# The output projection of an attention and SwiGLU kernel as seven block products instead of eight, with an order of work written out in full

## The chip, the cores and the metric

The kernel runs on one core of one Trainium2 chip. The metric is the device time of one execution in microseconds (us); the kernel before takes 381.37 us, the median of three runs (381.36 to 381.74). PE is TensorE (matrix products), DVE is VectorE, ACT is ScalarE, POOL is GpSimd, SP is SyncE, which here only issues transfers.

## The reference, cut to what matters

Attention with a decay for 8 batches of 8 heads, 576 tokens and 64 columns per head; its output, seen as 4608 tokens of 512 columns, goes through an RMS norm and a gated feed-forward layer. The change concerns the last product alone.

```
scores = scale * q @ k.T + decay; causal mask; softmax; attn @ v     # 8 x 8 heads, 576 tokens
xn = x / rms * rms_g                                                 # 4608 x 512
silu * val = silu(xn @ w_gate) * (xn @ w_val)                        # 4608 x 1536
out = (silu * val) @ w_out                                           # 4608 x 512
```

## The kernel before, in words

**Two halves, woven together.** The attention half works batch by batch. It loads q, k and v through POOL's queue, turns q and k (DMA transposes on SP's queue, the first ones on PE), and scales v (`scale_v`, L444, on DVE for the first two batches and on POOL for the others). Scores are matrix products into the two `sc` banks (L469), ACT takes the exponential (L487), POOL masks the diagonal block (`affine_select`, L494), PE multiplies by v (L513), DVE divides by the row sum (L527, L529), and `norm` makes the normed rows and turns them (L545 to L578).

The feed-forward half works on 9 groups of 512 tokens. Groups 0 to 7 are the first 512 tokens of the batches, group 8 gathers the last 64 tokens of all eight. `gate` (L615) makes one 128-column slice of the hidden layer for 512 tokens: four matmuls with `w_gate` and four with `w_val` (L624), each with 128 partitions, a 128-column stationary operand and 512 moving columns; a tanh on ACT (L636); two element-wise steps on DVE (L638 makes `ga`, L631 writes the slice of `hT` in bf16). There are 12 slices per group. In groups 0 and 1 a unit is 16 matmuls of 128 moving columns, so that the work can begin with the first 128 tokens. The norm's gains are multiplied into the weights on the way (L358, DVE).

`project` (L643) is the part that is changed. For 128 tokens it sums 12 matmuls in one PSUM bank: `hT` is the stationary operand (128 by 128) and `wo` the moving one (512 columns). The 12 come in three parts of four. ACT copies the bank to `ores` (L662), and SP's queue stores 128 tokens of 2 KB rows (L666, for group 8 L675). There are four such calls per group, 36 in all.

**Buffers.** All feed-forward products, and the values and transposes of the attention, share a ring of four PSUM banks `ff`. A gate slice takes two of them, one until L638 is done and one until L631 is done. `hT` has two buffers: a group's gates can't begin before the projection of the group two ahead of it has read its last block.

**What sets the order.** `Plan` (L41) holds every piece of work as a unit with an engine, an estimated duration, a key, its predecessors and the ring slots that it takes and gives back. `Plan.run` (L83) plays the units against these durations: an engine that is free takes the ready unit with the lowest key. The order in which units start there is the order in which instructions are written to each engine's queue, and the chip keeps that order on each engine. Before the play, 26 seeds shake the keys (L93 to L99). The durations steer the order only; on the chip an instruction waits for its real predecessors.

## Time and profile before

| What | Value |
|---|---|
| time, median of three runs | 381.37 us |
| span of the profiled execution, first to last instruction | 380.4 us |
| PE busy | 356.9 us in 3894 matmuls |
| DVE, ACT, POOL busy | 219.5, 237.9, 199.9 us |
| granted TensorE clock, mean | 0.996 |

The profiled execution's own time isn't given apart from its span; the span plus what lies around it (start and end of the execution) is what the runs time, and the median stands 0.97 us above the span. A row of the profile names a group of instructions by line, engine, operation and tiles, then how many there were, their busy time and mean duration, and after a bar the time for which the engine stood idle just ahead of them and what ended it. Matmuls are pipelined: a row's mean duration is longer than the distance at which they follow each other. In the table by stages, each engine has its busy time in that stretch and, in brackets, how many instructions.

### The profile page before, as it was taken

What the parts mean: (1) busy time and instruction counts of PE and PEld (TensorE: products, weight loads), DVE (VectorE), ACT (ScalarE), POOL (GpSimd) and SP (SyncE); (2) the same over time, 40 slices, a digit from 0 to 9 for tenths busy, and PEclk for the clock granted to TensorE, in tenths of its full rate; (3) what the DMA queues carried; (4) which work ended last, traced back from release to release, by engine and by line L of the source; (5) the groups of instructions that cost most, each with busy time, mean ns of one, the idle gap of its engine ahead of it and who ended that gap; (6) DMA issues with size and microseconds to landing.
All of it is one profiled execution on the core that took longest, in us unless ns stands there. A gap on an engine that the chain in (4) does not pass through costs nothing.

```text
span 380.4 us, 9641 instructions
## 1 busy us (share of the span) xinstructions
PE 356.9 (94%) x3894; PEld 213.6 (56%) x3942; DVE 219.5 (58%) x458; ACT 237.9 (63%) x378; POOL 199.9 (53%) x280
## 2 busy tenths in 40 slices
PE   2699999899979999999999999999999999999994
PEld 2489875698854455445555555555545544444441
DVE  6658999775645547454745565546654654554430
ACT  5676678789868576857695769566965443331321
POOL 8966589799998656964598449831302000000000
PEclk9999999999999999999999999999999999999998
DMA  9999999999999999993999499972120210100004
GB/s 124 211 215 212 218 136 216 160 156 159 151 142 141 154 115 134 178 161 62 137 150 173 80 138 143 179 92 56 36 57 30 55 34 29 55 28 29 28 30 110
DMA packets 128869, 44.84 MB, mean 118 GB/s; under 512 B 117300, under 2 KB 121912, under 8 KB 128824
## 3 DMA queue, kind: packets, MB, share of 16 engines
q0 software_dynamic: 76368, 23.34, 62.1%
q1 hardware_dynamic: 52376, 20.74, 30.2%
q8 instruction: 31, 0.51, 0.6%
q10 hardware_dynamic: 80, 0.13, 0.2%
q14 instruction: 14, 0.11, 0.1%
HBM read 37.90 MB, written 9.44 MB: 124 GB/s over the span
## 4 chain that ended last, share of the span: by engine, by line
PE 81%; DVE 7%; DMA 6%; POOL 3%; issue 2%; ACT 1%; POOLq 0%; ACTq 0%
PE ff L624 45%; PE ff L649 22%; PE ff L513 7%; PE sc L469 6%; DMA v<-in_v_dram 3%; DMA qk<-in_q_dram 2%; DVE wg L358 2%; DVE x L529 1%; DVE wv L358 1%; DVE hT L631 1%; POOL v L339 1%; DVE Vs L444 1%; DVE Vs L445 1%; DVE ga L638 1%; POOL qk L328 0%
## 5 line engine op out<-in xcount | busy, mean ns | idle before, releaser
L638 DVE SCALAR_TENSOR_TENSOR ga<-th,ff 128x512 f32<-128x512 f32 x108 | 73.5, 683 | 85.2 <-ACT th L636 83.7
L636 ACT ACTIVATE th<-ff 128x512 f32<-128x512 f32 x108 | 64.2, 595 | 73.0 <-PE ff L624 56.6
L649 PE MATMUL ff<-wo,hT 128*128 128x512 bf16 x409 | 105.3, 379 | 0.8 <-issue 0.2
L487 ACT ACTIVATE PT<-sc 128x1024 bf16<-128x1024 f32 x96 | 95.0, 1017 | 9.9 <-PE sc L469 9.7
L624 PE MATMUL ff<-xT,wg 128*128 128x128 bf16 (+1 forms) x655 | 97.2, 288 | 3.7 <-issue 1.9
L624 PE MATMUL ff<-xT,wv 128*128 128x128 bf16 (+1 forms) x665 | 96.9, 287 | 1.7 <-DVE x L529 0.8
L631 DVE SCALAR_TENSOR_TENSOR hT<-ga,ff 128x512 bf16<-128x512 f32 x108 | 72.9, 684 | 19.6 <-PE ff L624 17.0
L624 PEld LDWEIGHTS <-wg 128*128 128x128 bf16 x720 | 54.0, 99 | 39.1 <-issue 2.9
L624 PEld LDWEIGHTS <-wv 128*128 128x128 bf16 x720 | 53.2, 98 | 36.7 <-issue 1.3
L649 PEld LDWEIGHTS <-hT 128*128 128x128 bf16 x432 | 40.5, 98 | 45.5
L494 POOL TENSOR_SCALAR_AFFINE_SELECT PT<-PT 128x1024 bf16<-128x1024 bf16 x32 | 35.6, 1112 | 49.2 <-ACT PT L487 49.2
L513 PEld LDWEIGHTS <-PT 128*128 128x128 bf16 x896 | 37.9, 99 | 12.7 <-POOL PT L494 0.2
L513 PE MATMUL ff<-Vs,PT 128*128 128x65 bf16 x896 | 42.6, 195 | 0.1
L444 POOL TENSOR_TENSOR Vs<-v,decT 128x512 bf16<-128x512 f32 (+1 forms) x30 | 31.4, 1048 | 15.7 <-DMA v<-in_v_dram 14.0
L662 ACT COPY ores<-ff 128x512 f32<-128x512 f32 (+1 forms) x36 | 20.9, 580 | 29.8 <-PE ff L649 29.0
L469 PE MATMUL sc<-QT,KT 64*128 64x128 bf16 (+1 forms) x960 | 34.1, 213 | 2.5 <-ACT PT L487 1.7
L339 POOL DMA_DIRECT2D v<-in_v_dram x39 | 34.5, 887 | 2.9 <-DVE rden L527 1.1
L529 DVE TENSOR_TENSOR x<-ff,rden 128x256 f32<-128x256 f32 (+1 forms) x80 | 33.8, 422 | 2.8
L469 PEld LDWEIGHTS <-KT 64*128 64x128 bf16 x960 | 24.6, 96 | 15.0 <-issue 11.5
L527 DVE RECIPROCAL rden<-ff 128x4 f32<-128x4 f32 (+1 forms) x80 | 14.1, 176 | 30.5 <-PE ff L513 30.5
L545 ACT ACTIVATE junk<-x 128x512 bf16<-128x512 f32 (+1 forms) x40 | 25.1, 627 | 9.7 <-DVE x L529 8.9
L316 POOL DMA_DIRECT2D qk<-in_q_dram x34 | 29.9, 882 | 1.8 <-DMA qk<-in_k_dram 0.9
(63 smaller groups left out, 221.3 us busy)
## 6 DMA issues: line engine op xcount, KB each, us to landing
out_dram<-ores SPq DMA_DIRECT2D x32, 256.0 KB, 3.8
v<-in_v_dram POOLq DMA_DIRECT2D x31, 256.0 KB, 6.0
qk<-in_k_dram POOLq DMA_DIRECT2D x26, 128.0 KB, 5.6
qk<-in_q_dram POOLq DMA_DIRECT2D x26, 128.0 KB, 4.8
wv<-in_moe_w_val_dram POOLq DMA_DIRECT2D x3, 512.0 KB, 13.0
wg<-in_moe_w_gate_dram POOLq DMA_DIRECT2D x3, 512.0 KB, 11.2
wo<-in_moe_w_out_dram POOLq DMA_DIRECT2D x2, 768.0 KB, 16.1
v<-in_v_dram POOLq DMA_DIRECT2D x8, 128.0 KB, 7.6
```

The source lines that it names most:

```text
L339: queue.dma_start(out=T_v32[h.slot][0:n, :, :], in_=v[b, :, p0:p0 + n, :].rearrange("h p d -> p h d"))
L444: eng.tensor_tensor(T_Vs[hv.slot][0:n, j, :, 0:D], T_v32[h.slot][0:n, :, :], bcast(dj, D), ALU.mult)
L469: nc.tensor.matmul(t[:, par, c:c + n], lhsT=kt[r, p, kj * 128:(kj + 1) * 128], rhs=qt[r, p, qi * 128:qi * 128 + n], start=True, stop=True)
L487: nc.scalar.activation(T_of_p[hp.slot][:, 0:2 * half].rearrange("p (a c) -> p a c", a=2)[:, :, 0:cols], T_sc[h.slot][:, :, 0:cols], ACT.Ex ...
L494: nc.gpsimd.affine_select(out=d, in_=d, pattern=[[0, 8], [1, n]], compare_op=ALU.is_ge, fill=0.0, base=0, channel_multiplier=-1)
L513: nc.tensor.matmul(po[:, p, :], lhsT=T_of_p[h.slot][:, c:c + 128], rhs=vs[:, kj, 2 * p + par, :], start=(kj == 0), stop=(kj == qi))
L529: nc.vector.tensor_tensor(d, po[:, :, 0:D], bcast(r, D), ALU.mult)
L624: nc.tensor.matmul(T_ff[h.slot][:, c:c + n], lhsT=w[:, dc, fc * 128:(fc + 1) * 128], rhs=xT[:, dc, t0:t0 + n], start=(dc == 0), stop=(dc = ...
L631: nc.vector.scalar_tensor_tensor(hT, in0=three[0], scalar=0.5, in1=three[1], op0=ALU.mult, op1=ALU.mult)
L636: th = act(0.6, key - 0.1, lambda: nc.scalar.activation(T_th[ht.slot], T_ff[hg.slot], ACT.Tanh, scale=0.5), [ug], take=[ht])
L638: a = dve(0.69, key - 0.1, lambda: nc.vector.scalar_tensor_tensor(T_ga[ha.slot], in0=T_th[ht.slot], scalar=1.0, in1=T_ff[hg.slot], op0=ALU ...
L649: nc.tensor.matmul(T_ff[hf.slot], lhsT=T_hT[hold_hT[g].slot][:, fc, j * 128:(j + 1) * 128], rhs=wo[:, fc, :], start=(fc == 0), stop=(fc == ...
```

## The change

**The product.** For each group of 512 tokens the hidden block (512 tokens by 1536) is cut into 2 by 2 blocks of 256 tokens by 768, and `w_out` into 2 by 2 blocks of 768 by 256. Seven block products replace eight. Each is 12 matmuls of 256 moving columns: two halves of 128 tokens, 6 slices of the hidden dimension, both halves in one PSUM bank. DVE makes four sums or differences of hidden blocks per group (`s1` to `s4`, each 128 partitions by 1536 elements, bf16, from SBUF to SBUF; `s3` overwrites a block of `hT`) and once, for the whole kernel, four of weight blocks (`combine`). The results are put together as they leave PSUM: two copies on ACT and five additions of an SBUF tile and a bank on DVE (`plus`). Two products are summed onto a bank that has been copied out already (`m2` on `m1`, `m3` on `m5`).

**The stores.** A store now takes 256 tokens by 256 columns, in rows of 1 KB, four per group (group 8: eight). All go through SP's queue; before, the very last one went through ACT's.

**The order.** The seeds are gone. `ORDER` gives each of the 1797 units its rank as two letters, in the order in which units are created, and the play uses the ranks as keys. Ring slots and predecessors are as before, `ores` has five buffers instead of three, and a ring `sm` of three holds the block sums. Some estimated durations are set anew: loads through POOL, and the weights' scaling at 2.0 instead of 1.3.

**A shared tile.** The buffers `qk2`, which the first two batches use to turn q and k on PE, now lie inside the tile `wt` that later takes the combined weights.

```diff
-SEEDS = (37914, 460032, 76309, 917069, 999632, 56819, 902762, 379427, 333574, 378073, 410848, 600471, 719706,
...
+LETTERS = string.digits + string.ascii_letters
+ORDER = (
+    "0e1q020d000b0c080j0406030i0a0u0w0l0m0q0r0x090o0E0H0I070p010h050g0f0t0k0y0n0J0s0O0v0T0F1b0K1e0A0W0P1h"
...
+        for u, a, b in zip(self.units, ORDER[::2], ORDER[1::2]):
+            u.key = LETTERS.index(a) * len(LETTERS) + LETTERS.index(b)
...
+    wt = sb.tile([128, 3, NFC // 2, DM // 2], BF16, name="wt")
+    flat = wt.rearrange("p k f d -> p (k f d)")
+    T_qk2 = [flat[:, i * 1024:(i + 1) * 1024].rearrange("p (h r d) -> p h r d", h=H, r=2) for i in range(sizes["qk2"])]
...
+    T_sm = ring("sm", sizes["sm"], [128, NFC // 2, GT // 2], BF16)
...
-            Lw[nm, i] = [dve(1.3, key, emit, deps[nm])]
+            Lw[nm, i] = [dve(2.0, key, emit, deps[nm])]
...
+    def combine(deps):
+        def add(name, out, a, b, *need):
+            Lt[name] = dve(0.95, 0.85, lambda: nc.vector.tensor_tensor(out, a, b, ALU.subtract), list(need))
+        add("t1", wt1, w12, w11, Lo[0], *deps)
+        add("t3", w12, w22, w12, Lo[1], Lt["t1"])
+        add("t2", wt2, w22, wt1, Lt["t1"], Lo[1])
+        add("t4", wt4, w21, wt2, Lt["t2"])
...
-    def project(g, j, key):
...
+    def project(g, key, sums):
...
+        def s1():
+            nc.vector.tensor_tensor(T_sm[h1.slot], blocks()[2], blocks()[3], ALU.add)
...
+        u1 = dve(0.95, sums, s1, done[1], take=[h1], give=[hs])
+        u3 = dve(0.95, sums + 0.001, s3, [u1] + done[0], give=[hs])
+        u2 = dve(0.95, sums + 0.002, s2, [u1] + done[0], take=[h2], give=[hs, h1])
+        u4 = dve(0.95, sums + 0.003, s4, [u2], take=[h4], give=[hs, h2])
...
+        def product(a, w, hf, deps, take=(), give=(), more=False):
+            def emit():
+                t = T_ff[hf.slot]
+                for s in range(2):
+                    for fc in range(HF):
+                        nc.tensor.matmul(t[:, s * HD:(s + 1) * HD], lhsT=a()[:, fc, s * 128:(s + 1) * 128],
+                                         rhs=w[:, fc, :], start=(not more and s == 0 and fc == 0), stop=(s == 1 and fc == HF - 1),
...
+            return pe(1.315, key(n[0] - 1), emit, deps, take=list(take), give=list(give))
...
+        m1 = product(lambda: blocks()[0], w11, f1, done[0] + [Lt["t1"]], take=[f1], give=[hs])
+        v1 = copy(f1, A, [m1], take=[A])
+        m2 = product(lambda: blocks()[1], w21, f1, done[0] + [v1, Lo[1]], give=[hs], more=True)
+        store(E, 0, 0, copy(f1, E, [m2], take=[E], give=[f1]))
+        m6 = product(lambda: T_sm[h2.slot], wt2, f2, [u2, Lt["t2"]], take=[f2], give=[h2])
+        v2 = plus(f2, A, A, [m6, v1], give=[f2])
+        m7 = product(lambda: blocks()[2], w12, f3, [u3, Lt["t3"]], take=[f3], give=[hs])
+        v3 = plus(f3, A, Bb, [m7, v2], take=[Bb], give=[f3])
+        m5 = product(lambda: T_sm[h1.slot], wt1, f4, [u1, Lt["t1"]], take=[f4], give=[h1])
+        v4 = plus(f4, Bb, C, [m5, v3], take=[C])
+        store(C, 1, 1, v4)
+        m3 = product(lambda: T_sm[h4.slot], w22, f4, [m5, v4, u4], give=[h4], more=True)
+        store(A, 0, 1, plus(f4, A, A, [m3, v3], give=[f4]))
+        m4 = product(lambda: blocks()[3], wt4, f5, done[1] + [Lt["t4"]], take=[f5], give=[hs])
+        store(Bb, 1, 0, plus(f5, Bb, Bb, [m4, v4], give=[f5]))
```

## The prediction on record

> **What bounds the kernel now.** I read the page first: how busy each engine is, and which of them the chain that ended last runs through.
>
> ```profile
> span 380.4 us, 9641 instructions
> ...
> PE 356.9 (94%) x3894; PEld 213.6 (56%) x3942; DVE 219.5 (58%) x458; ACT 237.9 (63%) x378; POOL 199.9 (53%) x280
> ...
> PE 81%; DVE 7%; DMA 6%; POOL 3%; issue 2%; ACT 1%; POOLq 0%; ACTq 0%
> PE ff L624 45%; PE ff L649 22%; PE ff L513 7%; PE sc L469 6%; DMA v<-in_v_dram 3%; DMA qk<-in_q_dram 2%; DVE wg L358 2%; DVE x L529 1%; DVE wv L358 1%; DVE hT L631 1%; POOL v L339 1%; DVE Vs L444 1%; DVE Vs L445 1%; DVE ga L638 1%; POOL qk L328 0%
> ```
>
> PE is on the chain for 81% of the span, and the line that is changed (L649) for 22%. An average hides stages, so the table by stages comes next. Its columns are the stretch, its length, and the busy time of PE, PEld, DVE, ACT and POOL.
>
> ```profile
> 0.00:10.30 10.30, 3.57 (x38) 2.71 (x38) 6.18 (x26) 5.62 (x7) 9.10 (x17) 1.00 1.19 141
> 10.30:39.00 28.70, 24.73 (x434) 22.31 (x432) 19.93 (x44) 19.28 (x30) 21.11 (x29) 1.00 1.35 208
> 39.00:76.50 37.50, 33.95 (x622) 26.64 (x623) 33.27 (x74) 28.14 (x41) 28.33 (x35) 1.00 1.71 182
> 76.50:141.00 64.50, 62.06 (x914) 43.94 (x920) 36.88 (x80) 50.21 (x83) 56.04 (x81) 1.00 1.44 145
> 141.00:180.00 39.00, 38.66 (x377) 20.52 (x384) 21.43 (x44) 27.61 (x44) 26.27 (x36) 1.00 1.09 135
> ...
> 297.00:364.70 67.70, 67.33 (x343) 31.36 (x349) 35.85 (x57) 22.24 (x39) 0.73 (x2) 1.00 0.12 40
> 364.70:380.40 15.70, 10.66 (x49) 4.67 (x48) 1.59 (x3) 2.13 (x4) 0.00 (x0) 0.91 0.28 68
> ```
>
> From 141 us to 364.7 us PE has no gaps worth naming (38.66 of 39.00, 67.33 of 67.70), at full clock (1.00). Before that it loses 3.97, 3.55 and 2.44 us in the three stages behind the first 10.3 us. In the stage from 39 us DVE is the crowded engine: 33.27 of 37.50 us. The chain in order of time gives the period of one batch and one group in the steady stretch:
>
> ```profile
> 141.02 3.62 PE ff L624 x16
> ...
> 180.06 3.62 PE ff L624 x16
> ```
>
> The same piece comes back after 39.04 us. So there, what leaves PE leaves the time, as long as no other engine gets 39 us of work or makes PE wait.
>
> **Part 1: PE's work.** Matmuls overlap, so a price is the distance of starts, not the duration of one. In the timeline, eight matmuls of 512 columns, and then 32 of 128 columns:
>
> ```profile
> 328.63 1.89 PE L624 MATMUL ff<-xT,wg 128*128 128x512 bf16 x8
> 330.35 1.89 PE L624 MATMUL ff<-xT,wv 128*128 128x512 bf16 x8
> ```
>
> ```profile
> 98.89 1.96 PE L624 MATMUL ff<-xT,wg 128*128 128x128 bf16 x32
> 100.69 1.95 PE L624 MATMUL ff<-xT,wv 128*128 128x128 bf16 x32
> ```
>
> A 512-column matmul takes (330.35 - 328.63) / 8 = 0.215 us, a 128-column one (100.69 - 98.89) / 32 = 0.0563 us. How many are removed, a group row of the weight loads says (some matmul records are missing, the loads are all there):
>
> ```profile
> L649 PEld LDWEIGHTS <-hT 128*128 128x128 bf16 x432 | 40.5, 98 | 45.5
> ```
>
> Removed: 432 x 0.215 = 92.9 us. Added: 9 groups x 7 products x 12 = 756 matmuls of 256 columns. The trace has none of that width. Bounds: half a 512-column one, 0.1075 us (81.3 us in all), and two 128-column ones, 0.1125 us (85.1 us). The straight line between the two rows gives 0.0563 + 128 x (0.215 - 0.0563) / 384 = 0.1092 us; I take that: 1.31 us a product, 82.6 us in all. **PE: -10.3 us** (ends -11.6 and -7.8), or -1.15 us a group. The 324 added weight loads cost nothing beyond that, since 128-column matmuls, each with its own load, follow each other at 0.056 us; only a load that isn't pulled ahead would cost its 98 ns.
>
> **Part 2: DVE's work.** New on DVE are four sums a group, four weight sums once, and five evictions a group that add an SBUF tile to a bank. ACT loses two of four copies a group, which nobody waits for. In the groups by line and form:
>
> ```profile
> L631 DVE SCALAR_TENSOR_TENSOR hT<-ga,ff 128x512 bf16<-128x512 f32 x108 | 72.9, 684 | 19.6 <-PE ff L624 17.0 <-remote 0.4
> ...
> L529 DVE TENSOR_TENSOR x<-ff,rden 128x256 f32<-128x256 f32 x64 | 27.1, 424 | 2.2
> ...
> L575 DVE COPY xT<-ff 128x512 bf16<-128x512 bf16 x4 | 1.6, 415 | 0.5 <-PE ff L565 0.5
> ```
>
> An eviction is of L631's kind (a tile, a bank, 512 elements): 5 x 0.684 = 3.4 us a group. For a sum of two bf16 tiles in SBUF there is no row. Two-input rows give (684 - 424) / 256 = 1.016 ns an element and 164 ns fixed: 1536 elements take 1.72 us at that rate. L575 moves 512 bf16 elements in 415 ns, which is about half the time per element behind the same fixed part; at half the rate a sum takes 164 + 780 = 0.94 us. I take 0.94, the bf16 row, since all operands of the sums are bf16 while the two-input rows have f32 in them; 1.72 stays as the other end. By the Trainium skill, page "VectorE: DVE Perf Modes", section "The perf-mode tier table", a two-tensor operation on 16-bit SBUF operands goes at two elements a cycle (1224 ns for 2048), which makes an estimate of 0.96 us; no run here shows it yet, and it would change the sum by nothing that counts.
>
> Per group: 4 x 0.94 + 3.4 = 7.2 us. In the steady period DVE goes from 21.43 of 39.0 us to 28.6 of 37.9 us, 76% (84% with the long sums). DVE doesn't become the bound by its total. What is left is a sum standing in front of a gate's step on DVE, behind which two banks of the ring of four wait, and then PE. How much room there is, the group of L638 within 76.5 to 364.7 us says:
>
> ```profile
> L638 DVE SCALAR_TENSOR_TENSOR ga<-th,ff 128x512 f32<-128x512 f32 x94 | 64.2, 684 | 80.5 <-ACT th L636 79.2
> ```
>
> DVE waits 80.5 / 94 = 0.86 us ahead of each such step: a 0.94 us sum nearly fits into one of these gaps, and a stretch of products asks little of DVE (0.69 us per 1.31 us of PE). **Middle: +1.0 us** for sums that don't fit, ends 0 and 5.8 (the second rival).
>
> **Part 3: the head.** The weight sums (3.8 us) and group 0's 7.2 us fall on DVE near the stage from 39 us, which has 37.50 - 33.27 = 4.2 us left there. If all 11.0 had to fit in, PE would be 6.8 us late; put behind 76.5 us (DVE 36.88 of 64.5) they cost nothing. The ranks of `ORDER`, laid over the order in which units are created, put four of group 0's products behind the first gates of group 1, so part of it is late enough. The planner's new durations and the shared `qk2` tile can move the head both ways. **+0.6 us**, ends -3.3 (a third of the 9.96 us that PE loses in those three stages) and +6.8.
>
> **Part 4: the tail.** The end of the timeline, and the store's row:
>
> ```profile
> 375.49 0.37 ACT L662 COPY ores<-ff 128x256 f32<-128x256 f32 x1 [0.28 <-PE ff L649]
> 375.89 0.42 DVE L662 COPY ores<-ff 128x256 f32<-128x256 f32 x1 [10.02 <-ACT ores L662]
> 376.35 0.58 ACTq L675 DMA_DIRECT2D out_dram<-ores  x1
> ```
>
> ```profile
> L675 SPq DMA_DIRECT2D out_dram<-ores x7: 466/547/590, 370.0 to 376.4; - x7
> ```
>
> Now the last bank leaves in two halves, one after the other (375.49 to 376.31: 0.82 us), and two queues issue side by side. Then, one eviction of 0.68 us and two issues on SP, the second 0.55 us behind the first: -0.14 + 0.55 = **+0.4 us**. In front of that, group 8's sums need the last slice of `hT`; the ranks put a product of group 7 (1.31 us) between the last gate and group 8's first product, and another one near the end, so I book no gap (other end: 1.2 us, the step L631 and its wait). The stores' rows of 1 KB instead of 2 KB cost nothing: in the last stages the transfers are at 0.12 to 0.28 of the engines.
>
> **Sum.** -10.3 + 1.0 + 0.6 + 0.4 = -8.3 us. The profiled span of 380.4 us becomes 372.1; the median of the runs, 381.37, lies 0.97 above that span, so 373.1 us. A difference of 0.2% (0.8 us) is about what a measurement of this kernel can tell from none.
>
> **The rivals.**
>
> *An early gain besides.* A new order may also recover PE's gaps ahead of 141 us. Against it: most of the early gaps hang on loads, and DVE gets fuller there. With a third of the 9.96 us back: 373.1 - 0.6 - 3.3 = 369.2 us.
>
> *Sums and POOL stand in each other's way.* In the timeline a mask on POOL starts while a DVE operation with two SBUF inputs runs:
>
> ```profile
> 9.20 0.68 DVE L444 TENSOR_TENSOR Vs<-v,ff 128x512 bf16<-128x512 f32 x1
> ...
> 9.79 1.17 POOL L494 TENSOR_SCALAR_AFFINE_SELECT PT<-PT 128x1024 bf16<-128x1024 bf16 x1
> ```
>
> ```profile
> L494 POOL TENSOR_SCALAR_AFFINE_SELECT PT<-PT 128x1024 bf16<-128x1024 bf16 x4 | 4.5, 1114 | 7.2 <-ACT PT L487 7.2
> ...
> L444 POOL TENSOR_TENSOR Vs<-v,decT 128x512 bf16<-128x512 f32 x4 | 4.2, 1050 | 0.0
> ```
>
> POOL reads SBUF for at least 4.5 + 4.2 = 8.7 us of a 39 us period, 22%. Of the 24 sums in groups 1 to 6 some 5 would meet such an operation, and if each lost a whole one (1.1 us) to PE it is 5.8 us instead of my 1.0: 377.9 us. For it: the sums are the first frequent DVE operations with two SBUF inputs. Against it: PE would have to feel every one in full. The Trainium skill, page "SBUF — State Buffer", section "Who interferes with whom", says that a DVE instruction with two SBUF inputs and a POOL instruction that reads SBUF exclude each other, the later one waiting in full. It speaks against this change; the mask above, begun 0.09 us ahead of the DVE operation's end, took 1.17 us against a mean of 1.11, which is no more than a hint of such a wait.
>
> *Slower: sums at one element a cycle.* Then each of 36 sums is 0.78 us longer than I take it, 28 us in all, and doesn't fit into the 0.86 us gaps. If half reaches PE: 373.1 + 14 = 387.1 us. It decides from 8.3 / 28 = 30% on. For it: every two-input row in the trace runs at that rate. Against it: those rows have f32 operands, and DVE would still be at 84%.
>
> *Slower: narrow matmuls are paced by their loads.* If the 324 added loads each showed their 98 ns, +31.8 us: 404.9 us. The rows at 128 columns contradict it. The Trainium skill, "TensorE: Matmul & The Clock Gate", section "Back-to-back issue gap", gives a sustained 81 ns at 128 columns and 131 ns at 512. By it (estimate: 98 ns at 256) the projection would go from 56.6 to 74 us, and the change would lose 17 us. Both rows here differ from it (56 and 215 ns), and the measurement decides.
>
> *All eaten up.* Several small waits add up to the gain, and nothing is to be seen: 381.4 us.
>
> **How the numbers follow.** Forecast 0.60, early gain 0.12, POOL 0.14, long sums 0.09, loads 0.02, eaten up 0.03. The first three are faster: 0.86; same 0.03; slower 0.11. The range runs from 369.0 (the early gain) to 378.5 (POOL's case with the upper matmul price half counted); it leaves out 0.14 above and some 0.05 below. The forecast's own range is 371 to 376.
>
> **What would show it.** Right: 756 loads in the projection, products of 12 matmuls 1.31 us apart, sums of 0.94 us, a period of 37.9 us with PE still at 99%, masks at their 1.1 us. Wrong: sums near 1.7 us; PE idle ahead of `ff` or projection matmuls released by DVE; a POOL or DVE operation stretched where a sum runs beside a mask; PE gaps between 39 and 76.5 us well over 3.55 us; PE idle between the last gate and group 8's products.

## The result, and the profile after

The changed kernel takes 378.31 us (median of 7 runs, 376.9 to 382.27), the kernel before on the same chip 381.37 us (380.71 to 381.78): a ratio of 0.9927, with a 95% interval from 0.9901 to 0.9954. It is faster by 3.1 us where 8.3 us were forecast. The range of the prediction holds the time, by 0.2 us at its upper end; the forecast of 373.1 us is 5.2 us off. Run again on another chip, the same kernel took 380.79 us, a ratio of 0.9978 [0.9952, 1.0005]: above the range, and not clear of no gain at all. On the first chip the changed kernel varies by 5 us from run to run and the kernel before by 1 us; on the chip of the second run they vary by 4.6 and 4.1 us, so the wider spread is clear on the first chip alone. (Two executions in the runs below, of 1283 and 1325 us, are three times as long as all the others and are left out of the ranges.)

The profiled execution of the changed kernel took 376.9 us, the fastest of its seven. From its page:

```profile
span 375.2 us, 10418 instructions
...
PE 348.3 (93%) x4266; PEld 244.9 (65%) x4266; DVE 290.9 (78%) x542; ACT 225.9 (60%) x360; POOL 207.5 (55%) x280
```

DVE has got the work that was forecast (219.5 to 290.9 us), and PE has lost some. The table by stages has the same cuts as the one in the prediction, and the last stage moved to the new end:

```profile
10.30:39.00 28.70, 25.94 (x475) 23.51 (x474) 21.34 (x48) 22.76 (x34) 22.61 (x31) 1.00 1.44 212
39.00:76.50 37.50, 31.89 (x629) 28.93 (x625) 34.32 (x66) 26.31 (x40) 27.61 (x33) 1.00 1.68 157
76.50:141.00 64.50, 61.34 (x961) 48.01 (x958) 52.47 (x103) 47.13 (x77) 59.55 (x82) 1.00 1.46 168
141.00:180.00 39.00, 38.34 (x463) 24.68 (x461) 29.78 (x58) 27.49 (x46) 26.69 (x35) 1.00 1.08 126
...
219.00:258.00 39.00, 37.82 (x398) 24.17 (x399) 30.32 (x50) 23.16 (x36) 23.23 (x33) 1.00 0.97 142
...
364.70:375.20 10.50, 5.26 (x49) 4.46 (x46) 4.04 (x6) 0.00 (x0) 0.00 (x0) 0.88 0.49 125
```

PE now idles for 37.50 - 31.89 = 5.61 us from 39 to 76.5 us (3.55 before) and for 3.16 us from 76.5 to 141 us (2.44 before). The steady stretch has small holes too: 1.18 us from 219 to 258 us, where it had 0.37 us. The row of the kernel before:

```profile
219.00:258.00 39.00, 38.63 (x378) 20.48 (x384) 21.44 (x44) 27.57 (x45) 24.43 (x34) 1.00 1.11 135
```

The idle share hides PE's real losses, because matmuls overlap. So I added up, over all pairs of neighbouring matmuls in a trace, the distance of their starts beyond the pace of that shape (216 ns for 512 columns, 109 for 256, 56 for 128, less for narrower ones). What is left of PE's time is its work. The trace of the kernel before lacks 48 matmul records and that of the last version 34 (their weight loads are there), so these two columns hang on how such holes are counted, and are good to about half a us. In us:

| Where | before | after | after, on another chip | last version (`port_wo_early`) |
|---|---|---|---|---|
| PE's work at full pace | 341.97 | 331.87 | 331.87 | 331.66 |
| ahead of the first matmul | 5.49 | 7.73 | 7.73 | 7.73 |
| lost up to 40 us | 12.58 | 9.32 | 9.63 | 9.64 |
| lost from 40 to 100 us | 7.84 | 12.10 | 17.55 | 10.25 |
| lost from 100 to 120 us | 2.58 | 0.84 | 0.81 | 2.18 |
| lost from 120 us on | 4.94 | 8.10 | 8.17 | 6.11 |
| from the last matmul's end to the end | 4.97 | 5.20 | 5.17 | 5.20 |
| span | 380.4 | 375.2 | 380.9 | 372.8 |

The work falls by 10.1 us by this table; from the counts, 432 x 0.216 - 756 x 0.109, it is 10.9 us. The forecast was 10.3. Two losses grow: from 120 us on, by 3.2 us in both executions, and from 40 to 100 us, by 4.3 us in the one and 9.7 us in the other. The first is the same in both profiled executions, the second differs. (The last version's profiled execution, 374.46 us, is the slowest of its five.)

**The loss from 120 us on.** A sum beside POOL, in the timeline of the changed kernel, first DVE and then POOL (start, duration):

```profile
149.14 1.83 DVE L708 TENSOR_TENSOR hT<-hT 128x1536 bf16<-128x1536 bf16 x1
150.89 0.94 DVE L711 TENSOR_TENSOR sm<-sm,hT 128x1536 bf16<-128x1536 bf16 x1
```

```profile
149.12 1.04 POOL L495 TENSOR_TENSOR Vs<-v,decT 128x512 bf16<-128x512 f32 x1
150.10 0.94 POOL L496 CAST Vs<-decT 128x8 bf16<-128x8 f32 x1
```

POOL begins to scale v 0.02 us ahead of the sum on L708, and the sum takes 1.83 us: the 1.0 us of the scaling, and then 0.9 us of its own. POOL's next instruction, on 8 columns, lasts 0.94 us (to 151.04), until just behind the end of the sum on L708 (150.97). The sum and POOL's two operations go one after the other. All 36 sums take 40.6 us, 1.13 us each on average; those that meet no such POOL operation take 0.95, but for one of 1.80 us at 214.61 that stands beside two load issues on POOL alone, and that stays unexplained.

**The loss from 40 to 100 us.** The waits of PE in that stretch, first in the profile of after, then in that of its second run (how long in all, how many, the longest):

```profile
PE ff L616 <- ACT xn L608: 2.5, 2, 2.3
PE ff L675 <- DVE hT L682: 2.2, 3, 0.9
```

```profile
PE ff L616 <- ACT xn L608: 5.3, 1, 5.3
PE ff L675 <- DVE hT L682: 3.2, 3, 2.3
```

It is the same wait for batch 1's normed rows, 2.3 us in one execution and 5.3 us in the other. In the kernel before it was short:

```profile
PE ff L565 <- ACT xn L557: 0.5, 2, 0.3
```

Followed back in the second run, on POOL, ACT and PE:

```profile
62.18 0.89 POOL L351 DMA_DIRECT2D qk<-in_q_dram  x1 [4.44 <-DMA qk<-in_k_dram]
63.13 0.19 POOL L600 TENSOR_SCALAR ms<-sq 128x2 f32<-128x2 f32 x1
63.41 0.72 POOL L601 TENSOR_TENSOR rs<-ms,mhalf 128x2 f32<-128x2 f32 x1
```

```profile
64.16 1.33 ACT L608 ACTIVATE xn<-x,rs 128x512 bf16<-128x512 f32 x2 [5.24 <-POOL rs L601]
```

```profile
64.94 1.22 PE L616 MATMUL ff<-ident,xn 128*128 128x128 bf16 x8 [5.34 <-ACT xn L608]
```

POOL stands for 4.44 us in front of the issue of a load for batch 2, until an earlier transfer has landed; the small norm step, which is ready, is queued behind it; ACT waits for that step, and PE for ACT. And behind PE's gap the clock goes down. The same run's table in pieces of 5 us (the granted clock is the third number from the end):

```profile
60.00:65.00 5.00, 0.06 (x1) 0.07 (x2) 0.72 (x3) 0.84 (x2) 2.67 (x4) 0.84 2.86 99
65.00:70.00 5.00, 5.00 (x34) 3.98 (x35) 2.82 (x7) 2.92 (x5) 4.98 (x7) 0.50 1.50 158
70.00:75.00 5.00, 5.00 (x114) 4.68 (x113) 3.73 (x7) 2.80 (x5) 2.74 (x5) 0.98 1.89 188
```

PE is called busy from 65 to 70 us, but at a clock of 0.50 and with 34 matmuls. In the faster execution the gap was half as long and the clock stayed at 1.00.

### The profile page after: what moved, and what is told of

It reads as the page before. It is cut to its first block, busy times and chain, and to the rows that moved or that the text cites. A ratio compares the mean times of both kernels' runs of the same rounds, so it can differ in the third digit from the quotient of the medians.

```text
span 375.2 us, 10418 instructions
## 1 busy us (share of the span) xinstructions
PE 348.3 (93%) x4266; PEld 244.9 (65%) x4266; DVE 290.9 (78%) x542; ACT 225.9 (60%) x360; POOL 207.5 (55%) x280
## 5 line engine op out<-in xcount | busy, mean ns | idle before, releaser
L675 PE MATMUL ff<-xT,wg 128*128 128x128 bf16 (+1 forms) x672 | 96.2, 289 | 3.0 <-DVE hT L682 1.6
L729 PEld LDWEIGHTS <-hT 128*128 128x128 bf16 x432 | 41.4, 98 | 7.3 <-issue 0.2
L739 DVE TENSOR_TENSOR ores<-ores,ff 128x512 f32<-128x512 f32 x45 | 30.6, 684 | 17.0 <-PE ff L729 12.9
L729 PE MATMUL ff<-wo,hT 128*128 128x256 bf16 x324 | 39.5, 273 | 0.0
L608 ACT ACTIVATE xn<-x,rs 128x512 bf16<-128x512 f32 (+1 forms) x40 | 27.8, 719 | 13.0 <-POOL rs L601 12.9
L729 PEld LDWEIGHTS <-sm 128*128 128x128 bf16 x324 | 30.9, 98 | 6.7 <-issue 2.0
L351 POOL DMA_DIRECT2D qk<-in_k_dram x34 | 29.6, 879 | 4.5 <-DMA wo<-in_moe_w_out_dram 3.4
```

What stands on the lines that cost most here:

```text
L675: nc.tensor.matmul(T_ff[h.slot][:, c:c + n], lhsT=w[:, dc, fc * 128:(fc + 1) * 128], rhs=xT[:, dc, t0:t0 + n], start=(dc == 0), stop=(dc = ...
L729: nc.tensor.matmul(t[:, s * HD:(s + 1) * HD], lhsT=a()[:, fc, s * 128:(s + 1) * 128], rhs=w[:, fc, :], start=(not more and s == 0 and fc = ...
L739: return dve(0.69, key(n[0] - 1) - 0.05, lambda: nc.vector.tensor_tensor(T_ores[to.slot], T_ores[a.slot], T_ff[hf.slot], ALU.add), deps, **kw)
```

## The experiments

Each run stands beside runs of the kernel before on its chip; the ratio is to those. The expectations number the theories as they came up. Of the later loss: theory 1, the sums and POOL's operations exclude each other; theory 2, it is the sums' own length. Of the early loss: theory 3, it comes from the new order, by POOL's queue in particular (3a); theory 4, DVE is too full; theory 5, the sum of the transfers paces the stage; rival 6, it is the written order whatever the transfers do; rival 7, it is the place of the `wo` loads in that order.

### The same kernel again, without the sums, and with little work for POOL

`after_again` is the changed kernel. `no_sums` leaves the sums out, and the products read blocks of `hT` in place of them:

```diff
-            nc.vector.tensor_tensor(T_sm[h1.slot], blocks()[2], blocks()[3], ALU.add)
+            pass
...
-        m6 = product(lambda: T_sm[h2.slot], wt2, f2, [u2, Lt["t2"]], take=[f2], give=[h2])
+        m6 = product(lambda: blocks()[0], wt2, f2, [u2, Lt["t2"]], take=[f2], give=[h2])
```

`small_pool` cuts POOL's scaling of v and its masks, from batch 2 on, to one column per head; `before_small_pool` does so to the kernel before:

```diff
-            eng.tensor_tensor(T_Vs[hv.slot][0:n, j, :, 0:D], T_v32[h.slot][0:n, :, :], bcast(dj, D), ALU.mult)
+            w = D if b < 2 else 1
+            eng.tensor_tensor(T_Vs[hv.slot][0:n, j, :, 0:w], T_v32[h.slot][0:n, :, 0:w], bcast(dj, w), ALU.mult)
...
-                def mk(hp=hp, n=n, T_of_p=T_of_p):
+                def mk(hp=hp, n=n if b < 2 else 1, T_of_p=T_of_p):
```

> The changed kernel itself, to see how far its executions differ and to have a second profile. Its first seven runs went from 376.9 to 382.3 us, those of the kernel before only from 380.7 to 381.8 us. If the spread is its own, five more runs scatter over more than 2 us again and the ratio to the kernel before is 0.990 to 0.995; if it was chance, they lie within 1 us.

> The changed kernel without its 36 block sums of hidden blocks: the products read blocks of hT instead, all else and the whole order stay as they are (the four weight sums too). Theory 1, sums and POOL operations that read SBUF exclude each other, and DVE then comes late: the 3 us that PE loses more than before between 120 and 300 us go, and 1 us or so of the early loss: 374 to 375.5 us. Theory 2, the sums' own length on DVE: the same time. Theory 3, the loss is one of the new order ahead of 100 us and has nothing to do with the sums: 377.5 to 378.5 us, PE's loss after 120 us unchanged.

> The changed kernel with POOL's scaling of v cut to one column per head and its masks to one column per head, both from the third batch on (these parts of v and of the masking are left out); sums, order and waits stay. Theory 1: the sums of groups 1 to 6 go back from 1.0 to 1.8 us to 0.95 us, DVE is in time, PE's extra loss after 120 us goes: 374.5 to 376 us, less what the kernel before gains from the same cut. Theory 2: sums at 0.95 us or not, the time stays within 0.7 us of the changed kernel's. Theory 3: no change.

> The kernel before with the same cut of POOL's work from the third batch on, as a control. PE has no waits for POOL after 120 us there, so under all theories the time stays within 0.7 us of 381.4 us; if it falls by 2 us or more, the cut itself is worth that much and has to be taken off the other run.

Measured, with the kernel before at 381.53 us: `after_again` 380.79 us, 0.9978 [0.9952, 1.0005]; `no_sums` 377.09 us, 0.9882 [0.9848, 0.9916]; `small_pool` 375.34 us, 0.9823 [0.9783, 0.9863]; `before_small_pool` 380.94 us, 0.9987 [0.9961, 1.0014]. `no_sums` falls between the times that theories 1 and 3 gave it. Less work on POOL is worth 5.5 us to the changed kernel, 2.9 of them from 120 us on, and 0.6 us to the kernel before (the runs of `small_pool` go from 373.3 to 381.4 us; the profiled one took 378.9). A group of sums, in the profile of after and in that of `small_pool`:

```profile
L708 DVE TENSOR_TENSOR hT<-hT 128x1536 bf16<-128x1536 bf16 x9 | 11.2, 1240 | 0.0
```

```profile
L709 DVE TENSOR_TENSOR hT<-hT 128x1536 bf16<-128x1536 bf16 x9 | 8.6, 951 | 0.0
```

And what PE makes of it, in the table by stages of `small_pool`:

```profile
219.00:258.00 39.00, 39.00 (x421) 26.43 (x419) 28.46 (x52) 23.75 (x37) 17.07 (x35) 1.00 1.29 155
```

The sums are at 951 ns, and PE's 1.18 us of idle time there are gone. Without the sums, and with little on POOL, the loss from 120 us on is 5.3 us in both, against 8.2 with them. That settles the later loss: 3 us, by exclusion. The early loss stays in both (16.2 and 13.2 us from 40 to 100 us), so it is another matter.

### The norm ahead of the loads

The chain at 60 us goes through POOL's queue. `norm_first` issues the loads of batches 2 and 3 behind batch 1's norm; `norm_first_small_pool` has both edits.

```diff
+    for u in late[2, 2][2:] + late[2, 3] + late[2, 4] + late[3, 0] + late[3, 1]:
+        rs_of[1, 0].then.append(u)
+        u.need += 1
```

> The changed kernel with one edit in the order: loads of batches 2 and 3 that stood in POOL's queue ahead of the norm of batch 1's first two blocks are issued behind it. In both profiles of the changed kernel POOL stood 2.4 to 4.4 us in front of such a load (until an earlier load landed), the norm waited behind it, and PE stood 2.4 to 5.5 us at about 60 us; in the slower execution the granted clock was 0.50 right after. Theory 3a, this queue at POOL makes both the early loss and the spread: PE's gap at 60 us goes to under 1 us, the median is 377 to 378.5 us (the changed kernel had 378.3 and 380.8), the spread over runs under 2 us. Theory 1 (sums and POOL): median and spread stay, since the sums after 120 us still meet POOL.

> The same edit of the order, and POOL's scaling of v and its masks cut to one column per head from the third batch on (that part is left out). If sums against POOL (theory 1) and the queue at POOL (theory 3a) are separate causes and add up, this is 3 us below the run with the edit alone: 374 to 375.5 us, PE's loss after 120 us at 5 us as in the kernel before. If they are one and the same, it is no faster than POOL's cut alone was (375.3 us).

Measured, before at 381.27 us: `norm_first` 380.45 us, 0.9961 [0.9931, 0.999]; with less work on POOL 377.31 us, 0.9917 [0.9879, 0.9954]. A miss. PE's waits from 55 to 90 us in `norm_first`:

```profile
PE sc L520 <- DMA KT<-qk: 3.5, 1, 3.5
PE ff L730 <- DVE ores L740: 2.7, 1, 2.7
```

The wait for `xn` is gone, and PE waits for a later `KT` instead, since the loads are later by that much. That wait alone isn't the cause. The 3.1 us between the two runs are about the later loss once more, though the second run too missed the time that was expected of it.

### Plain keys

`no_order` drops the use of `ORDER`, so that the products are played with the keys that the code gives them; `before_no_seeds` drops the seeds from the kernel before.

```diff
-        for u, a, b in zip(self.units, ORDER[::2], ORDER[1::2]):
-            u.key = LETTERS.index(a) * len(LETTERS) + LETTERS.index(b)
```

> The seven products with the plain keys: ORDER isn't applied, and no seeds shake the keys. If the written order carries the gain, this is 5 us or more slower than the changed kernel, 384 us or above. If the products alone make the gain, it is within 3 us of the changed kernel.

> The kernel before with the plain keys, the seeds left out. Beside the seven products with plain keys it gives what the products are worth when neither order was searched. If PE's 10 us count in full there too, the products are 8 to 10 us faster than this one; if DVE and POOL take it back as they do in the changed kernel, 0 to 5 us. The seeds themselves should be worth 2 to 10 us: 384 to 392 us.

Measured, before at 381.27 us: 391.43 us, 1.0276 [1.0244, 1.0309], and 387.45 us, 1.0163 [1.0131, 1.0194]. With plain keys on both sides, seven products are 4 us slower than eight, where they were expected to be faster or equal: the change's gain is there only with an order made for it. The written order is worth 11 to 13 us to the products, the seeds 6 us to the kernel before.

### Less for DVE early, and an order that knows of the exclusion

`no_weigh` leaves out the 24 operations that multiply the gains into the weights, `before_no_weigh` does the same to the kernel before. `late_weigh` does them after group 1's gates instead of after group 0's. `port` leaves all work as it is and gives the planner a ring of one slot, `port`, which each sum, each mask and each of POOL's scalings of v hold, so that it books them one after the other.

```diff
-                for dc in range(NDC):
-                    nc.vector.tensor_scalar_mul(w[:, dc, c0:c1], w[:, dc, c0:c1], rgT[:, dc:dc + 1])
+                pass
```

```diff
+        po = [Hold("port", 1) for _ in range(4)]
-        u1 = dve(0.95, sums, s1, done[1], take=[h1], give=[hs])
+        u1 = dve(0.95, sums, s1, done[1], take=[h1, po[0]], give=[hs, po[0]])
...
-                masked[b, qi].append(pool(0.15 + 0.95 * n / 128, key, mk, [e]))
+                px = Hold("port", 1)
+                masked[b, qi].append(pool(0.15 + 0.95 * n / 128, key, mk, [e], take=[px], give=[px]))
```

> The changed kernel without the 24 operations on DVE that multiply the norm's gains into the gate weights (this scaling is left out); order and waits stay as they are. They take some 14 us of DVE between 45 and 75 us, where DVE is at 92% in the changed kernel. Theory 4, the early loss (12 to 18 us of PE between 40 and 100 us against 8 in the kernel before) comes from DVE being too full there for the weight sums, group 0's sums and the new evictions: gaps ahead of gate matmuls released by DVE shrink, PE's clock isn't halved any more ahead of 110 us, the loss falls under 8 us, and the median is 374 to 376 us with a spread under 2 us. Theory 5, the early gaps come from late transfers: the loss stays above 10 us and the median above 377 us.

> The kernel before with the same scaling left out, as a control: DVE is at 89% between 39 and 76.5 us there, PE loses 7.8 us between 40 and 100 us. Theory 4: at most 2 us faster (379.5 to 381 us), clearly less than the changed kernel gains. If it gains as much as the changed kernel, the scaling is a cost of both and doesn't explain the difference.

> The changed kernel with the gains multiplied into the normed rows of group 1 as well (as is done for group 0), and into the weights only behind group 1's gates, so that 14 us of DVE leave the stage from 45 to 75 us and fall behind 79 us. The plan is then no longer the one that the ranks were written for. Theory 4: PE's loss between 40 and 79 us falls by 3 us or more; the total is 375 to 379 us if the later place is free enough, and above 380 us if DVE is short there too or the order no longer fits.

> The changed kernel with a ring of one slot in the planner that a block sum on DVE, a mask on POOL and a scaling of v on POOL each hold while they run, so that the order no longer plans them at the same time; every instruction is the same. Theory 1: the sums' mean goes from 1.13 us towards 0.95 us, PE's loss after 120 us from 8 us to 5.5 us or so, and the time falls by 1 to 2.5 us against the changed kernel on the same chip. If it doesn't, the chip's engines drift too far from the plan for this to help, and the time is within 1 us of the changed kernel's.

Measured, before at 381.5 us: `no_weigh` 379.27 us, 0.9899 [0.9861, 0.9937], with runs from 374.67 to 384.41; `before_no_weigh` 380.8 us, 0.9989 [0.9963, 1.0014]; `late_weigh` 385.23 us, 1.0089 [1.0056, 1.0121]; `port` 376.35 us, 0.9886 [0.9847, 0.9925]. With a lighter DVE the loss from 40 to 100 us is still 14.0 us and the runs vary more, so DVE's fullness isn't the main cause either. `late_weigh` is a miss: 3.7 us slower than before. From 95 to 125 us PE waits there 4.3 us for ACT's `PT`; that the written ranks no longer fit is the likely reason, and wasn't tested. `port` lowers the later loss to 6.0 us (6.8 when run again, below) without taking any work away; the early one stays (12.6 us).

### A sixth of the output weights

Then the transfers. With the stretch from 30 to 75 us cut into 40 slices, the DMA engines are busy for 90% or more in all of them in the changed kernel's trace, and in all but two in that of the kernel before. `wo_small`, `before_wo_small` and `port_wo_small` load one block of 128 rows of `w_out` per load instead of six, and all products read that block (in the changed kernel the weight sum `t3` then gets a tile of its own); the order of the work stays. `port_again` is `port`.

```diff
-                    out=wo[:, i * 6:(i + 1) * 6, :],
-                    in_=moe_w_out[i * 768:(i + 1) * 768, :].rearrange("(c p) f -> p c f", p=128))
+                    out=wo[:, i, :],
+                    in_=moe_w_out[i * 768:i * 768 + 128, :])
```

> The changed kernel with only a sixth of the output weights loaded: each of the two loads of wo brings one block of 128 rows instead of six, and all products read that block in place of the six (their sums are not the right ones any more; the place that t3 is written to is a tile of its own). The order of the work on every engine is that of the changed kernel; some 1.3 MB less are moved while the DMA engines are busy in every slice from 30 to 75 us, which is about 7 us of their time at 170 to 190 GB/s. Theory 5 (the early stage is paced by its transfers, and PE work that is saved there comes back as waits for them): the PE time lost between 40 and 100 us falls from 12 to 18 us to under 9, the spread between runs becomes under 2 us, and the time falls by 4 to 8 us against the changed kernel, to 371 to 375. Rival 6 (the early waits come from the written order itself, engine behind engine, whatever the transfers do): it stays within 1.5 us of the changed kernel, 377 to 381, and the gaps at 55 to 95 us stay.

> Control: the kernel before with the same sixth of wo loaded and read. Theory 5: it gains too, for its transfers are as full there, but less, since its PE lost only 7.8 us between 40 and 100 us: 1 to 4 us, to 377.5 to 380.5, so that the two kernels without these transfers stand 5 to 7 us apart instead of 3. Rival 6: within 1 us of the kernel before, 380.5 to 382.

> The changed kernel with both: the planner keeps block sums apart from masks and v scaling (as in the run named port), and only a sixth of wo is loaded. If the early loss and the loss by the sums are separate and both are cured, this gives what the prediction's PE term alone would give: 371 to 373.5. Theory 5 has it 3 to 5 us under port; rival 6 within 1.5 us of port.

> The run named port once more, on the chip of these three, so that they are compared with it and its spread is known: 375.5 to 377.5, all theories alike; about 2 us under the changed kernel and 5 us under the kernel before.

Measured, before at 381.67 us: `wo_small` 375.77 us, 0.9838 [0.9807, 0.9869]; `before_wo_small` 380.7 us, 0.9981 [0.9959, 1.0004]; `port_wo_small` 371.87 us, 0.9744 [0.9716, 0.9773]; `port_again` 377.61 us, 0.9899 [0.9864, 0.9934]. Beside `port` the transfers of wo are worth 5.7 us, to the kernel before 1.0, which is where rival 6 had it. The six runs of `port_wo_small` lie within 1.6 us (371.34 to 372.98). With both losses cured, the changed kernel stands 8.8 us below the kernel before with the same edit: the forecast gain is there. In `wo_small` alone the early loss fell less than theory 5 wanted (11.7 us instead of under 9, with a time 0.8 us above the range it gave), so it was open whether it is all the bytes or these two loads.

### The two loads of wo, earlier

The two loads stand late in the changed kernel. Their issues, before and after (the two starts are first and last):

```profile
L364 POOL DMA_DIRECT2D wo<-in_moe_w_out_dram x2: 822/829/836, 19.1 to 32.6; - x2
```

```profile
L399 POOL DMA_DIRECT2D wo<-in_moe_w_out_dram x2: 852/857/862, 36.9 to 41.8; - x2
```

And what follows the second one on POOL in after (issues of loads alone):

```profile
41.81 0.86 POOL L399 DMA_DIRECT2D wo<-in_moe_w_out_dram  x1
42.63 1.60 POOL L351 DMA_DIRECT2D qk<-in_k_dram  x2
44.19 0.93 POOL L351 DMA_DIRECT2D qk<-in_q_dram  x1
...
47.17 1.83 POOL L374 DMA_DIRECT2D v<-in_v_dram  x2
49.44 0.88 POOL L351 DMA_DIRECT2D qk<-in_q_dram  x1 [0.43 <-DMA qk<-in_q_dram]
...
52.30 0.90 POOL L351 DMA_DIRECT2D qk<-in_k_dram  x1
56.59 0.69 POOL L351 DMA_DIRECT2D qk<-in_k_dram  x1 [3.39 <-DMA wo<-in_moe_w_out_dram]
```

Eight issues (wo, two k, q, two v, q, k), and the ninth waits 3.39 us for the first one's transfer. The plan has eight lanes for POOL's transfers (`sw=8`), and the count fits: the long wo transfer holds one of them while POOL's queue runs full behind it. Another number of lanes wasn't tried. `wo_early` moves the two loads forward with the same bytes: the first takes the rank of a load of k for batch 2, the second the first one's, and that load of k the second one's. The play then also moves some other pieces a little. `port_wo_early` does that to `port`.

```diff
             u.key = LETTERS.index(a) * len(LETTERS) + LETTERS.index(b)
+        x, y, z = self.turns
+        x.key, y.key, z.key = z.key, x.key, y.key
...
+    P.turns = [late[2, 1][1], *wo_at]
```

> The changed kernel with the two loads of wo issued earlier: the first takes the place in the order of batch 2's load of k block 1, the second the first one's, and that load of k the second one's (planned 31 and 35 us instead of 35 and 41; the kernel before issues them at 19 and 33). All the same transfers, so theory 5 with its full meaning (the sum of the transfers paces the stage) says that it doesn't help: the time stays within 2 us of the changed kernel, 377 to 381, and POOL's waits ahead of loads between 50 and 68 us only go to another transfer. Rival 7 (it is the place of wo among the loads, late and with POOL's queue behind it): POOL's wait of 3.4 us for wo is gone, PE's wait at 60 us is under 0.5 us as in the kernel before, and the time is 2 to 4 us less, 374 to 376.

> The same edit on the run named port. Theory 5: within 2 us of port, 375 to 379. Rival 7: 2 to 4 us less than port, 372.5 to 375, which would be the fastest kernel that computes the reference.

Measured, before at 381.13 us: `wo_early` 375.95 us (375.4 to 376.93), 0.9863 [0.984, 0.9887]; `port_wo_early` 372.86 us (372.11 to 374.46), 0.9776 [0.975, 0.9801]. Theory 5, that the sum of the transfers sets the pace, falls: the same bytes moved forward do nearly all that five sixths fewer did (372.86 against 371.87 us). POOL's waits from 50 to 68 us, in after and in `wo_early` (the whole answer for the latter):

```profile
POOL qk L351 <- DMA wo<-in_moe_w_out_dram: 3.4, 1, 3.4
POOL qk L351 <- DMA qk<-in_k_dram: 2.4, 1, 2.4
```

```profile
POOL PT L548 <- ACT PT L541: 1.2, 1, 1.2
```

POOL stands in front of no load any more, and PE's wait for `xn` is gone. But the early stages of `wo_early` aren't free of loss:

```profile
39.00:76.50 37.50, 34.60 (x647) 30.87 (x644) 35.96 (x77) 26.66 (x41) 27.41 (x33) 0.95 1.72 163
76.50:141.00 64.50, 61.93 (x941) 48.76 (x943) 49.58 (x94) 47.11 (x76) 59.14 (x82) 0.97 1.24 166
```

PE idles for 2.90 and 2.57 us instead of 5.61 and 3.16, and the clock falls to 0.50 twice (at 64.6 and 85.1 us). Its profiled execution, 376.06 us, is only 0.8 us faster than that of the changed kernel; the gain is in the median.

`port_wo_early` leaves nothing out, takes 8.3 us less than the kernel before, and is the best version found. Its early stages:

```profile
39.00:76.50 37.50, 32.98 (x636) 29.32 (x634) 35.73 (x75) 27.02 (x40) 27.58 (x32) 1.00 1.79 160
76.50:141.00 64.50, 61.60 (x960) 48.20 (x964) 50.09 (x96) 47.00 (x76) 60.20 (x82) 1.00 1.33 167
```

PE still idles for 4.52 and 2.90 us there, with waits of 1 to 2 us for DVE in place of those on POOL; what these would cost to remove wasn't tried.

## Why the prediction was right or wrong

**Part 1, PE's work: right.** 10.1 us less by the table and 10.9 by the counts, forecast 10.3. The last products of the changed kernel, and the weight loads of the projection:

```profile
365.87 1.47 PE L729 MATMUL ff<-wo,sm 128*128 128x256 bf16 x12
367.18 1.47 PE L729 MATMUL ff<-wt,hT 128*128 128x256 bf16 x12
368.49 1.47 PE L729 MATMUL ff<-wo,sm 128*128 128x256 bf16 x12
```

```profile
L729 PEld LDWEIGHTS <-hT 128*128 128x128 bf16 x432 | 41.4, 98 | 7.3 <-issue 0.2
L729 PEld LDWEIGHTS <-sm 128*128 128x128 bf16 x324 | 30.9, 98 | 6.7 <-issue 2.0
```

756 loads, and products 1.31 us apart: 0.109 us per matmul of 256 columns, the straight line between the two shapes. The rival of narrow matmuls is out, and with it the rule of the Trainium skill ("TensorE: Matmul & The Clock Gate", section "Back-to-back issue gap") by which the change would lose 17 us: the trace has 109 ns at 256 columns where that estimate had 98, and 216 ns at 512 where the page has 131.

**Part 2, DVE's work: the price of a sum was right, the term "Middle: +1.0 us" is the first step that failed.** A sum alone takes 0.95 us (forecast 0.94), so the rival of long sums is out. But the term measured 3.2 us, since I let the sums wait for room on DVE alone and put their meeting with POOL aside. The prediction's own rival, sums and POOL in each other's way, is the mechanism: it was given 5.8 us and a chance of 0.14, and is shown by `no_sums`, `small_pool` with its control, and `port`. What failed is the sentence against it, "PE would have to feel every one in full": the sums are 6.4 us longer in all (40.6 us against 36 x 0.95), and PE feels 3.2 of these, which is half, and still three times my term. The rule that the prediction cited from the Trainium skill, "SBUF — State Buffer", section "Who interferes with whom", holds to the letter for this pair of operations: 0.95 us alone, 1.83 us behind a POOL operation of 1.04 us. The mask of 1.17 us against 1.11 that I showed was no test of it: the operation on DVE beside it, `Vs<-v,ff`, reads one tile of SBUF and one PSUM bank, not two SBUF tiles.

**Part 3, the head: the second step that failed.** Forecast +0.6 us; up to 120 us it is +1.5 us in the fastest execution (-1.0 up to 40 us, and +2.5 behind it) and +7.2 us in the profiled one on the other chip. I costed DVE's new work in that stage and closed with "The planner's new durations and the shared `qk2` tile can move the head both ways". What was moved was never listed. The new ranks issue the two largest loads 9 to 18 us later, among the loads for batch 2; the second holds a lane of POOL's transfers while seven more are issued; and batch 1's norm stands in that queue. The ends -3.3 and +6.8 hold the +1.5 and just miss the +7.2, and they stood there for the wrong reason: DVE. That the place of these two loads is the main cause is shown by `wo_early` and `port_wo_early` with the same bytes, and by `port_wo_small` with the same order and fewer bytes; that `norm_first` and `no_weigh` didn't help shows that it is neither that one norm nor DVE's fullness alone. By which waits the loads cost PE time in each execution, and what makes up the loss that stays, is open.

The sign to look for was named rightly ("PE gaps between 39 and 76.5 us well over 3.55 us"): 5.61 us. That such a gap can also cost clock wasn't thought of.

The start was also costed at nothing, and is not: the first matmul begins at 7.73 us instead of 5.49. The rows, after and before:

```profile
7.73 0.69 PE L464 MATMUL ff<-ident,qk 128*128 128x128 bf16 x5 [7.73 <-DVE ident L299]
```

```profile
5.49 0.61 PE L415 MATMUL ff<-ident,qk 128*128 128x128 bf16 x4 [5.49 <-DMA qk<-in_k_dram]
```

It now waits for the identity instead of a load. POOL begins to make the identity at 6.76 us, behind six load issues, and at 3.29 us in the kernel before. With the plain keys of `no_order` the first matmul begins at 5.44 us, so this too is the written order. The losses up to 40 us fall by 3.3 us at the same time, so that it cancels; whether it could be had back wasn't tried.

**Part 4, the tail: right.** From the last matmul to the end 5.20 us instead of 4.97, +0.2 us against +0.4. No gap opens ahead of group 8's products.

**The offset from span to time: wrong by 0.7 us.** I set the median against the span of one profiled execution and got 0.97 us. In every run whose time is known beside its span it is 1.7 us (376.9 and 375.2; 382.6 and 380.9); the profiled execution of the kernel before was a slower one than its median.

**The upper end of the range: added up wrongly.** POOL's case is 377.9 us, and half of the upper matmul price is 1.25 us, which makes 379.1; 378.5 counts a quarter of it.

So of the 5.2 us between forecast and median, 0.7 are the offset and 2.2 the sums; PE's work (0.2 more, by the table) and the tail (0.2 less) cancel. Of the 2.3 left, 0.9 are the head in the profiled execution, and 1.4 lie between that execution and the median; I put these to the head too, since the later loss was the same in both profiles. With `port_wo_early`, which takes away part of both losses, the same forecast (373.1 us) would have been 0.2 us off its median, partly by luck: up to 120 us and from 120 us on its profile still loses 1.3 and 1.2 us more than the kernel before.

## What to carry to other kernels

When a change brings a new order, list what the order moves on every queue, above all the largest transfers and what stands behind them, before costing the arithmetic: here the place of two loads was worth about as much as the 36 new sums. When work moves from PE to DVE, count the DVE operations with two SBUF inputs and the POOL operations that read SBUF, and let the planner book them one after the other. If the executions of a kernel differ, look in the slower ones for a wait of some microseconds on PE with a lower clock behind it.

## What the runs showed of the hardware

A gap on PE can cost more than its length. In the second run of after, the granted clock was at 0.50 from 63.35 us, inside the gap of 5.3 us, to 70.18 us; in `wo_early` for 3.41 us behind a gap of 2.3 us at 83 us; in the first run of after, behind the one of 2.3 us, not at all. In the profile of the kernel before it is below 1 only behind the last products (from 377.71 us on). In all the traces here, each halved stretch ahead of the last products lasts 3.41, 6.83 or (in `no_order`) 10.24 us: once, twice or three times 3.41 us. The Trainium skill, "TensorE: Matmul & The Clock Gate", section "Part 1: The HAM clock gate", speaks of half the clock after an idle window of about 3.4 us that runs freely, not from the gap's start. The length of the stretches agrees with that. That PE has to be idle for a whole window doesn't: the clock fell behind gaps of 2.3 us, and in `wo_early` at 64.61 us with no gap over 0.82 us close ahead of it. What decides whether it falls stays open.

An instruction of 8 columns on POOL (L496) lasts 0.94 us where a sum runs beside it, and ends with that sum, while the same operation takes 0.22 us on average in the kernel before (L445), which has no sums. So the exclusion goes by whole operations and not by how much they read. A sum of 1536 bf16 elements takes 0.95 us, as the estimate in the prediction from the Trainium skill, "VectorE: DVE Perf Modes", section "The perf-mode tier table", had it (0.96).
